# Twelve small triangular inverses on VectorE: each elimination step as two whole instructions instead of four halves

## The chip, the cores and the metric

One core of one Trainium2 chip runs the whole program. The metric is the device time of one execution in microseconds (us). On the core TensorE (PE in the profile, its weight loads PEld) does the matrix products and transposes, VectorE (DVE) and ScalarE (ACT) the elementwise work and the eviction of PSUM, GpSimd (POOL) some products and some DMA issues, and SyncE (SP) most DMA issues.

## The reference, cut to what matters

For 4 batches of 8 heads a state matrix of 40x40 is updated 768 times, and the outputs of all heads, joined to rows of 320, go through a two-layer block with a softmax gate and a normalisation:

```python
for t in range(S):                                   # S = 768
    y[:, :, t] = np.einsum('bhd,bhde->bhe', rt, state)
    Sa = np.einsum('bhde,bhe->bhd', state, at)
    state = state * wt[:, :, None, :] - np.einsum('bhd,bhe->bhde', Sa, bt) \
            + np.einsum('bhd,bhe->bhde', vt, kt)
x = y.transpose(0, 2, 1, 3).reshape(B * S, H * D)    # 3072 x 320
h = x @ w_in; sm = softmax(h); solu = h * sm
out = (layer_norm(solu) * g_ln) @ w_out
```

## The kernel before, in words

The recurrence is worked in chunks of C = 64 steps of time. A chunk of all heads of two batches is one unit of the loop: N = 24 units, index i, two for each of the 12 chunks of the sequence. Within a chunk the rank-one corrections are coupled by a matrix that is the identity plus a strictly triangular part of 64x64, one for each head and batch. The kernel inverts its two diagonal blocks of 32x32 (Q = 32) directly on VectorE, and joins the two by products on TensorE (`couple`, line 548, and `close`, line 561).

**The inverse** is `invert` (line 495). One call serves two units (GRP = 2), so there are 12 calls, called n = 0 to 11 here, each with 64 blocks laid over 128 partitions, so that each partition holds half of the 32 columns of a block. The off-diagonal entries are brought from a DRAM scratch by `spread` (line 488) into tile `blk`, the result grows in tile `uu`, 16 columns of 32 entries on each partition. Step j, for j = 1 to 30, adds entry j of every column begun so far, times row j of `blk`, to the entries j+1 to 31. There are n_c = (j+1)//2 such columns on a partition and m = 31 - j entries. For n_c below 4 (j = 1 to 6) a step is n_c instructions of line 508. From j = 7 on a step is a product into the scratch tile `prod` (line 516) and a sum into `uu` (line 519), both done on two halves of the columns: product of the first half, product of the second, sum of the first, sum of the second. A half has at most 72 elements on a partition, which is the width of `prod`; `prod` has two buffers. The last step is followed by two DMAs of `uu` to DRAM (line 525, on SP), from where `bring` (line 529) fetches each unit's part, `flip` (line 542) transposes it on VectorE, and `couple` uses it.

**The order of the work** is written out by hand, for all engines: every engine runs its instructions in the order in which the program issues them. `invert` is a generator that yields after each step j. The loop over i (line 971) hands out a few steps at a time, in gaps between VectorE's other work, by the strings in `plans` (line 896): `vector("o2 2")` (line 232) runs two steps for a unit that needs its inverse soon, and then two of any. `some` (line 870) counts the steps. From i = 12 on the plan repeats every two units: entries 24 and 25 of `plans`. The letters b, s and f in a plan are stages of a conversion of the weights from 64-bit floats (`split`, line 188: DVE lines 196 and 197, then ACT lines 199 to 206, then DVE lines 208 to 210), which is done in the first 140 us.

**VectorE's other work in a unit**, in its order: `aT` (line 427) and `bT` (line 440), which evict transposes from the PSUM pair called A that the next transposes (`pst`, `pb`) then use; some steps of an inverse; `lu` (line 444, from the solve `pu`); a step or two; `psi` and `lv` (line 444, from the scores `ps`); `flip`; eight or nine steps; the row maximum `nmax` (line 761) of the wide product `h`; `tot` (line 710); the weighing of `e` (line 777), after ACT's exponential (line 769); `st` and `x` (lines 721 and 724). ACT then squares `e` (line 790), evicts `kvT` (line 583) and the output rows `osb` (line 859), and PE goes on to the transposes of the next unit.

Of the kernel before, what the change touches and what calls it, by code (L numbers as in the profile page):

```python
# [9 lines left out]
FP32 = mybir.dt.float32  # L10
# [7 lines left out]
P = 128  # L18
# [35 lines left out]
def kernel(  # L54
# [31 lines left out]
    two = ctx.enter_context(tc.tile_pool(name="two", bufs=2))  # L86
# [401 lines left out]
    def spread(n):  # L488
        nb = two.tile([P, Q, Q], FP32, tag="blk", name="blk")
        for y in range(2):  # L490
            queue = nc.gpsimd if n else nc.sync
            queue.dma_start(out=nb[C * y:C * y + C], in_=blocks[n].rearrange("e b s c -> (e b) s c"))
        return nb

    def invert(n):
        u = two.tile([P, Q // 2, Q], FP32, tag="uu", name="uu")
        flat = u.rearrange("p c t -> p (c t)")
        nc.gpsimd.memset(u[C:P], 0.0)
        nc.gpsimd.memset(flat[C:P, 1::Q + 2], 1.0)
        nb = spread(n)  # L500
        yield
        nc.vector.tensor_tensor(out=u[0:C], in0=nb[0:C, 0::2], in1=above, op=ALU.mult)
        nc.vector.memset(flat[0:C, 0::Q + 2], 1.0)
        for j in range(1, Q - 1):
            m, n_c = Q - 1 - j, (j + 1) // 2
            if n_c < 4:
                for c in range(n_c):
                    nc.vector.scalar_tensor_tensor(out=u[:, c, j + 1:Q], in0=nb[:, j, j + 1:Q], scalar=u[:, c, j:j + 1],  # L508
                                                   in1=u[:, c, j + 1:Q], op0=ALU.mult, op1=ALU.add)
            else:  # L510
                parts_ = ((0, n_c // 2), (n_c // 2, n_c))
                ts = []
                for lo, hi in parts_:
                    prod = two.tile([P, 72], FP32, tag="prod", name="prod")
                    ts.append(prod[:, 0:(hi - lo) * m].rearrange("p (c r) -> p c r", c=hi - lo))
                    nc.vector.tensor_tensor(out=ts[-1], in0=nb[:, j:j + 1, j + 1:Q].to_broadcast([P, hi - lo, m]),  # L516
                                            in1=u[:, lo:hi, j:j + 1].to_broadcast([P, hi - lo, m]), op=ALU.mult)
                for x, (lo, hi) in zip(ts, parts_):
                    nc.vector.tensor_tensor(out=u[:, lo:hi, j + 1:Q], in0=u[:, lo:hi, j + 1:Q], in1=x, op=ALU.add)  # L519
            if j < Q - 2:  # L520
                yield
        inverse[n] = dram.tile([Q, C, Q], FP32, tag="uu_dram", name="uu_dram")
        for y in range(2):
            queue = nc.sync
            queue.dma_start(out=inverse[n][y::2].rearrange("c b t -> b c t"), in_=u[C * y:C * y + C])
        yield
# [352 lines left out]
    def begin_inverse(n):  # L879
        steps.append((n, invert(n)))  # L880
        next(steps[-1][1])
# [285 lines left out]
```

## Time and profile before

| what | value |
|---|---|
| three runs | 541.44, 537.95, 540.57 us; median 540.57 |
| the profiled execution | 538.14 us, of which its span is 536.0 |
| mean granted TensorE clock in the span | 0.962 |
| VectorE | 426.4 us busy, 1752 instructions |
| of these, line 516 (products) | 576, 105.4 us |
| of these, line 519 (sums) | 576, 105.3 us |
| chain of work that ended last | PE 76%, DVE 7%, ACT 5%, DMA 4% |

The span runs from the first to the last instruction of the program. A group of instructions is given with its count, its busy time in us and the mean duration of one in ns; then the idle time of its engine just before it, and what ended it. In a timeline a line is one instruction or several alike in a row: start, time from the first one's start to the last one's end, engine, line, operation, output and inputs, and in brackets the idle time before it and what ended it. Where two instructions of one engine overlap in the records, the second has started before the first one's result is written.

### The profile page before, as it was taken

The numbers are of one execution on the slowest core, as the hardware profiler recorded it, in microseconds if no ns is written. First come the engines' busy times: TensorE is split into PE (matmuls) and PEld (weight loads), VectorE is DVE, ScalarE is ACT, GpSimd is POOL, SyncE is SP. The second block draws the span as 40 slices with busy tenths as digits, with TensorE's granted clock in tenths as the row PEclk, the third lists the DMA queues.
The fourth block names the chain that finished last, engine by engine and source line by source line (L and its number), as shares of the span: only waits on it lengthen the run. The fifth ranks groups of instructions, "written<-read, shape, count | busy, mean of one in ns | idle before, by whom it ended". The sixth has DMA issues, their size and how long they took to land.

```text
span 536.0 us, 28052 instructions
## 1 busy us (share of the span) xinstructions
PE 480.8 (90%) x12029; PEld 392.5 (73%) x12029; DVE 426.4 (80%) x1752; ACT 314.5 (59%) x627; POOL 218.9 (41%) x368
## 2 busy tenths in 40 slices
PE   4634566888989999999999999999999999999997
PEld 3524555666878878877887887788778877887766
DVE  4596998999988987997988979979989788544322
ACT  3734466668467666666656665676656555654433
POOL 4545546244253434636355363545354321210300
PEclk9998577789999999999999999999999999999999
DMA  7998879766456566675775675675554451421210
GB/s 144 158 145 165 191 136 206 167 134 137 77 124 125 107 135 124 134 147 103 144 154 114 115 146 122 123 151 107 114 122 101 95 125 43 106 64 29 61 53 24
DMA packets 198315, 63.95 MB, mean 119 GB/s; under 512 B 170936, under 2 KB 190496, under 8 KB 198192
## 3 DMA queue, kind: packets, MB, share of 16 engines
q1 hardware_dynamic: 185456, 42.26, 41.8%
q0 software_dynamic: 10384, 19.30, 14.3%
q8 instruction: 94, 1.54, 1.2%
q10 hardware_dynamic: 2352, 0.62, 0.7%
q14 instruction: 29, 0.24, 0.2%
HBM read 47.96 MB, written 14.16 MB: 116 GB/s over the span
## 4 chain that ended last, share of the span: by engine, by line
PE 76%; DVE 7%; ACT 5%; DMA 4%; SPq 3%; issue 2%; ACTq 0%; POOL 0%; POOLq 0%; DVEq 0%
PE po L285 20%; PE h L285 18%; PE px L285 7%; PE py L285 6%; PE pyo L285 6%; PE ps L285 3%; PE pu L285 3%; PE plnT L804 2%; DMA raw_w<-in_w_dram 2%; PE pa L400 2%; SPq L311 2%; PE pb L400 2%; PE pkv L400 2%; PE psr L285 2%; PE pcum L285 1%
## 5 line engine op out<-in xcount | busy, mean ns | idle before, releaser
L285 PE MATMUL h<-w_in,xT 64*64 64x512 f32 (+1 forms) x1064 | 121.3, 552 | 0.0
L285 PE MATMUL po<-w,lnT 128*128 128x160 f32 x768 | 115.2, 304 | 0.0
L285 PEld LDWEIGHTS po<-w,lnT 128*128 128x128 f32 x768 | 105.5, 190 | 4.7 <-issue 0.8
L516 DVE TENSOR_TENSOR prod<-blk,uu 128x48 f32<-128x48 f32 (+19 forms) x576 | 105.4, 223 | 1.4
L519 DVE TENSOR_TENSOR uu<-uu,prod 128x48 f32<-128x48 f32 (+19 forms) x576 | 105.3, 223 | 0.0
L483 POOL DMA_DIRECT2D nt_dram<-nt x86 | 51.0, 599 | 83.4 <-ACT nt L475 82.0
L792 POOL TENSOR_TENSOR rs<-var,mhalf 128x1 f32<-128x1 f32 x24 | 15.8, 658 | 137.0 <-ACT var L791 137.0
L761 DVE TENSOR_REDUCE nmax<-h 128x1 f32<-128x1024 f32 x24 | 29.3, 1220 | 32.6 <-PE h L285 32.6
L285 PEld LDWEIGHTS h<-w_in,xT 64*64 64x64 f32 x1064 | 36.7, 134 | 19.1 <-issue 15.5
L790 ACT ACTIVATE sq<-e,mu 128x1024 f32<-128x1024 f32 x24 | 26.9, 1119 | 23.9 <-DVE e L777 23.9
L444 DVE TENSOR_TENSOR lu<-pu,cst 128x512 f32<-128x512 f32 x24 | 16.5, 687 | 27.5 <-PE pu L285 27.2
L769 ACT ACTIVATE e<-h,nmax 128x1024 f32<-128x1024 f32 x24 | 26.7, 1111 | 17.1 <-DVE nmax L761 16.9
L558 ACT ACTIVATE wy<-py,cst 128x256 f32<-128x256 f32 x24 | 11.4, 474 | 40.3 <-PE py L285 40.3
L311 POOL DMA_DIRECT2D raw_r<-in_r_dram x48 | 33.3, 699 | 0.6 <-issue 0.6
L777 DVE SCALAR_TENSOR_TENSOR e<-h,e 128x1024 f32<-128x1024 f32 x24 | 29.2, 1218 | 3.7 <-ACT e L769 3.4
L393 POOL TENSOR_TENSOR kb<-raw_b,inv 128x320 f32<-128x320 f32 x24 | 21.2, 882 | 25.4 <-DMA raw_b<-in_b_dram 18.0
L285 PEld LDWEIGHTS py<-tu,nt 64*64 64x64 f32 x768 | 17.3, 145 | 18.8 <-issue 14.2
L508 DVE SCALAR_TENSOR_TENSOR uu<-blk,uu 128x30 f32<-128x30 f32 (+3 forms) x144 | 28.6, 252 | 1.5 <-DMA blk<-nt_dram 0.9
L617 ACT COPY st<-psr 128x416 f32<-128x416 f32 (+1 forms) x44 | 14.2, 375 | 26.1 <-PE psr L285 24.9
L285 PE MATMUL pcum<-lw,cst 128*128 128x160 f32 x48 | 14.7, 450 | 16.4 <-ACT lw L351 16.4
L285 PEld LDWEIGHTS py<-aT,bT 40*64 40x64 f32 x768 | 16.7, 152 | 14.5 <-issue 8.7
L285 PE MATMUL px<-st,aT 40*64 40x104 f32 x704 | 21.9, 263 | 5.9 <-DVE lv L444 5.8
(152 smaller groups left out, 1096.8 us busy)
## 6 DMA issues: line engine op xcount, KB each, us to landing
xT<-x_dram SPq DMA_DIRECT2D x48, 160.0 KB, 3.9
blk<-nt_dram POOLq DMA_DIRECT2D x22, 256.0 KB, 3.4
raw_w<-in_w_dram SPq DMA_DIRECT2D x48, 80.0 KB, 3.0
a<-in_a_dram SPq DMA_DIRECT2D x48, 80.0 KB, 3.2
raw_r<-in_r_dram POOLq DMA_DIRECT2D x48, 80.0 KB, 3.9
lv<-in_v_dram SPq DMA_DIRECT2D x48, 80.0 KB, 3.3
out_dram<-osb SPq DMA_DIRECT2D x46, 80.0 KB, 3.4
raw_b<-in_b_dram SPq DMA_DIRECT2D x44, 80.0 KB, 4.8
```

The costliest lines, as they stand in the source:

```text
L285: nc.tensor.matmul(o, lhsT=lhsT, rhs=rhs, start=start, stop=stop, skip_group_check=True)
L311: queue.dma_start(out=x[half(p), :, 0:D], in_=ap[2 * bp + p, :, ci * C:(ci + 1) * C, :].rearrange("h t d -> t h d"))
L393: nc.gpsimd.tensor_tensor(out=kb[:, j:j + H, 0:D], in0=d["raw_" + n], in1=heads(d["inv"]), op=ALU.mult)
L400: nc.tensor.transpose(out=t[0:W2, p, at + C * j:at + C * j + C], in_=x[half(p), 2 * j:2 * j + 2].rearrange("p a b -> p (a b)")[:, skip:ski ...
L483: queue.dma_start(out=blocks[n][e].rearrange("(a x h) s c -> a x s h c", a=GRP, x=2)[at, x], in_=nt[home:home + Q].rearrange("p h j c -> p ...
L508: nc.vector.scalar_tensor_tensor(out=u[:, c, j + 1:Q], in0=nb[:, j, j + 1:Q], scalar=u[:, c, j:j + 1], in1=u[:, c, j + 1:Q], op0=ALU.mult, ...
L516: nc.vector.tensor_tensor(out=ts[-1], in0=nb[:, j:j + 1, j + 1:Q].to_broadcast([P, hi - lo, m]), in1=u[:, lo:hi, j:j + 1].to_broadcast([P, ...
L519: nc.vector.tensor_tensor(out=u[:, lo:hi, j + 1:Q], in0=u[:, lo:hi, j + 1:Q], in1=x, op=ALU.add)
L761: nc.vector.tensor_reduce(out=nmax, in_=d["h"], axis=AX.X, op=ALU.max, negate=True)
L769: nc.scalar.activation(out=e, in_=d["h"], func=AF.Exp, bias=d["nmax"], accum_out=d["esum"])
L777: nc.vector.scalar_tensor_tensor(out=d["e"], in0=d["h"], scalar=1.0 / DFF, in1=d["e"], op0=ALU.mult, op1=ALU.mult, accum_out=d["mu"])
L790: nc.scalar.activation(out=pair("A" if i == N - 2 else "h", "sq").rearrange("p a b -> p (a b)"), in_=d["e"], func=AF.Square, scale=-float( ...
```

## The change

For j = 7 to 30 the columns are no longer cut in halves. A step is one product over all n_c columns and one sum over all of them. The scratch tile becomes 136 elements wide, since the largest step has 128 (j = 15: 8 columns of 16). Steps 1 to 6, the order of the steps, the plans and all other instructions stay. An inverse has 48 instructions of lines 516 and 519 instead of 96.

```diff
             else:
-                parts_ = ((0, n_c // 2), (n_c // 2, n_c))
+                parts_ = ((0, n_c),)
                 ts = []
                 for lo, hi in parts_:
-                    prod = two.tile([P, 72], FP32, tag="prod", name="prod")
+                    prod = two.tile([P, 136], FP32, tag="prod", name="prod")
                     ts.append(prod[:, 0:(hi - lo) * m].rearrange("p (c r) -> p c r", c=hi - lo))
                     nc.vector.tensor_tensor(out=ts[-1], in0=nb[:, j:j + 1, j + 1:Q].to_broadcast([P, hi - lo, m]),
                                             in1=u[:, lo:hi, j:j + 1].to_broadcast([P, hi - lo, m]), op=ALU.mult)
                 for x, (lo, hi) in zip(ts, parts_):
                     nc.vector.tensor_tensor(out=u[:, lo:hi, j + 1:Q], in0=u[:, lo:hi, j + 1:Q], in1=x, op=ALU.add)
```

## The prediction

> **What bounds the kernel now.** I read the busy times and the costliest groups first, then the engines by stretches, then the chain of work that ended last, then VectorE's timeline around the steps.
>
> ```profile
> PE 480.8 (90%) x12029; PEld 392.5 (73%) x12029; DVE 426.4 (80%) x1752; ACT 314.5 (59%) x627; POOL 218.9 (41%) x368
> ...
> L516 DVE TENSOR_TENSOR prod<-blk,uu 128x48 f32<-128x48 f32 (+19 forms) x576 | 105.4, 223 | 1.4
> L519 DVE TENSOR_TENSOR uu<-uu,prod 128x48 f32<-128x48 f32 (+19 forms) x576 | 105.3, 223 | 0.0
> ```
>
> The steps are half of VectorE's busy time. By stretches:
>
> ```profile
> core 0: us, PE busy (x) PEld busy (x) DVE busy (x) ACT busy (x) POOL busy (x), PEclk, DMA share, GB/s
> ...
> 50.00:100.00 50.00, 31.81 (x877) 29.08 (x881) 45.94 (x203) 25.56 (x54) 23.53 (x37) 0.64 0.82 171
> ...
> 250.00:300.00 50.00, 49.73 (x1321) 41.58 (x1312) 46.18 (x193) 31.67 (x63) 25.17 (x39) 1.00 0.64 127
> ```
>
> From 50 to 150 us PE has gaps and VectorE nearly none. From 165 us PE has none; VectorE, though 92% busy, waits for PE: in each pair of units about 2.2 us ahead of `lu` and 0.7 to 0.95 us ahead of one `nmax`. So the change counts in full only in the first stretch. The chain there runs through the steps:
>
> ```profile
> 68.22 0.67 DVE aT L427
> 68.89 0.34 DVE scale L196
> ...
> 105.38 0.60 DVE aT L427
> ...
> 113.11 0.61 DVE lv L444
> 113.85 1.67 PE px L285 x32
> ```
>
> What a step costs is a matter of starts. The first four lines here are steps 10 and 11 of the last inverse; then, from inverse 1, line 210 of a weight conversion reads what line 209 has just written, and an unrelated step follows:
>
> ```profile
> 436.65 0.34 DVE L516 TENSOR_TENSOR prod<-blk,uu 128x42 f32<-128x42 f32 x2
> 436.91 0.34 DVE L519 TENSOR_TENSOR uu<-uu,prod 128x42 f32<-128x42 f32 x2
> 437.29 0.35 DVE L516 TENSOR_TENSOR prod<-blk,uu 128x60 f32<-128x60 f32 x2
> 437.56 0.34 DVE L519 TENSOR_TENSOR uu<-uu,prod 128x60 f32<-128x60 f32 x2
> ...
> 74.71 0.68 DVE L209 SCALAR_TENSOR_TENSOR w_in<-bits,w_in 128x512 f32<-128x512 uint16 x1
> 75.43 0.69 DVE L210 TENSOR_TENSOR w_in<-w_in,bits 128x512 f32<-128x512 f32 x1
> 76.04 0.28 DVE L516 TENSOR_TENSOR prod<-blk,uu 128x28 f32<-128x28 f32 x2
> ```
>
> The unrelated step starts 0.61 us after line 210, whose duration is 0.69: about 83 ns before its end (`lv` after `psi`, and most such neighbours, have the same). Line 210 starts 0.72 us after line 209: 35 ns after its end. A result needed at once thus costs 118 ns more. Today's halves hide that: each reads a result made two instructions earlier, and a step of four takes 0.26 + 0.27 = 0.53 us. Only after steps 10, 14, 18, 22 and 26, where the cut moves by a column, does the next product read the sum just made: 0.38 instead of 0.26 us at 436.91.
>
> **The change part by part.** It removes 576 VectorE instructions and doubles the size of the other 576.
>
> The product over all columns is read at once by the sum, and the sum at once by the next product. So a step takes 2 x (d + 35 ns), d the duration of a whole-size instruction. None of 73 to 128 elements is in the trace; the nearest rows of the same engine and type are these:
>
> ```profile
> L519 DVE TENSOR_TENSOR uu<-uu,prod 128x72 f32<-128x72 f32 x12 | 2.7, 222 | 0.0
> ...
> L721 DVE TENSOR_TENSOR st<-tot,ex 104x160 f32<-104x160 f32 x40 | 11.2, 322 | 0.0
> ```
>
> A line between them has 1.14 ns per element; I take it, as it brackets the sizes. The small sizes alone (7 elements 171 ns, 72 elements 222) give 0.78, the low end; 1.14 is also the high end, since line 710 with 416 elements at 581 ns gives no more. Step 11 (6 x 20 = 120 elements): d = 222 + 48 x 1.14 = 277, after 2 x 312 = 623 ns, before 532: +90. Step 10 paid one dependence already: 634 to 589, -45. Step 30 (15 elements): 391 to 421. Done for all 24 steps, 12.40 us becomes 13.69: +1.29 us an inverse; with 0.78 ns it is +0.80. Where a run of steps ends and another instruction follows that reads nothing of it, the last 118 ns fall away. In the steady plan (runs 7-13, 14, 15-18, 19-27, 28-30) that leaves +0.36, -0.02, +0.28, +0.34, -0.02 = +0.94 us of VectorE's time for each pair of units. [...]
>
> Now what of it lies on the path.
>
> Inverse 0 (30 to 45 us): VectorE then waits 3.95 us for `blk`, and SP issues the DMA of `uu` at 47.5, 2.2 us after the last step: hidden. Without that cover it would be 1.2 us.
>
> Inverse 1: steps 7 to 22 run in one piece up to `aT` at 68.2: +1.02 us, and the conversion behind it is late, for which ACT waits; ACT's queue is then full up to the product `py` at 72.8, for which PE waits.
>
> ```profile
> 69.26 0.72 ACT L199 ACTIVATE scale<-scale,top 128x512 int32<-128x512 int32 x1 [0.86 <-DVE scale L196]
> ...
> 224.43 0.53 ACT L859 ACTIVATE osb<-po,rs 128x320 f32<-128x320 f32 x1 [0.32 <-PE po L285]
> ...
> 261.70 0.53 ACT L859 ACTIVATE osb<-po,rs 128x320 f32<-128x320 f32 x1
> ```
>
> Inverse 2: step 7 alone before `psi`, -0.04. Steps 8 to 15 (+0.36) are covered by VectorE's waits of 1.57 us for `tu` and 0.39 for ACT. Steps 16 to 18 before `aT` at 105.3, +0.18 (the load for `pst` starts 0.05 us after `aT` ends). Steps 19 to 25 before `lu`, `psi`, `lv` and PE's `px` at 113.9, +0.36. Inverse 3: five steps at 135 to 139 us before `nmax`, +0.16. Sum of the first stretch: 1.68 us.
>
> Later, PE's order is met late only where ACT's `kvT` and `osb`, which follow the weighing of `e`, have no wait left; the two rows of `osb` show a unit with 0.32 us left and one with none, at 261.7, where PE's unit took 18.76 us instead of 18.46. Steps 7 to 14 make `e` later by +0.34. At 262 and 337 us (no wait left) that is 2 x 0.34 = 0.68; in the four such units with 0.32 left 0.02 each, 0.08; at 187 us `bT` ends 0.13 us before PE's `pst` load: +0.21. In the others (0.6 to 0.7 left) nothing. In the other half of a pair, +0.28 and +0.34 end at a VectorE wait of 0.66 to 0.95 us ahead of `nmax`, and what is left at the wait of 2.2 us ahead of `lu`. The `uu` DMAs, issued up to 0.1 us later, feed `flip` some 12 us later; one wait of 0.68 us for them is seen. The wider scratch costs no instruction; half the instruction records save nothing on PE's path.
>
> Sum: 1.68 + 0.97 = 2.65 us, about +0.5%. The profiled execution took 538.14 us (span 536.0 and 2.1 around it), so 540.8 by its own account and a span of 538.7. It lies 2.4 us below the median, so against the median: 540.57 + 2.65 = 543.2.
>
> **The rivals.**
>
> *Dependence is free, fewer instructions win (faster).* If the next instruction started 83 ns before the end whatever it reads, step 11 would take 2 x (277 - 83) = 387 ns instead of 532 and an inverse 8.0 us instead of 12.4. The first stretch would gain 0.58 us at 68 us (the weights' DMA lands at 68.2, which then ends the wait), 0.16 at 90, 0.42 at 105, 1.17 at 109 and 0.90 at 139; the late units at 262 and 337 would get their 0.27 each back: -3.8 us, 536.8. Against it stand the 0.72 us of lines 209 and 210 (all thirteen such pairs have 34 or 35 ns after the end) and the jump at step 10. [...]
>
> *More of GpSimd's stalls fall into the steps (slower).* 36 of the 1152 step instructions last about 0.67 to 1.3 us longer, while GpSimd runs `kb` (line 393, 0.88 us) or issues DMAs; four of them, 2.7 us, in most pairs of units. If a longer run of dependent instructions catches one more, 0.67 us, ahead of `e` in each such half, ACT is late by 0.69 in four units, 1.01 in two, 0.4 and 0.3 in two: 5.5 us, with the first stretch 7.2: 547.8. For it: VectorE has no slack in those halves. Against it: a stall ends with GpSimd's instruction and each `kb` makes at most two, so their count should be GpSimd's and not VectorE's. It decides from about one extra stall for each pair.
>
> *The granted clock.* Between 49 and 117 us the clock goes between full and half in pieces of 3.4 us or multiples. If VectorE's later results move three of them to half, with PE 73% busy (90 to 100 us), that is 3 x 3.4 x 0.73 / 2 = 3.7 us more: 546.9; it can as well go the other way.
>
> **How the numbers follow.** The forecast 0.62, free dependence 0.10, more stalls 0.20, the clock 0.08. The forecast's own range: at the low end of d about a third of the sum, 541.4, and with the runs' own scatter (-2.6, +0.9) 538.8 to 545. Together with the stalls' 547.8 and their scatter the range is 538.5 to 549.5. About 1% is what a measurement of this kernel can tell from no change. Faster by over 1% is half of free dependence, 0.05; slower the stalls and most of the clock, 0.25; within 1% 0.70.
>
> **What would show it.** Lines 516 and 519 with 288 instructions each; products of 120 elements near 277 ns and starts 312 ns apart; step 11 near 0.62 us. VectorE's busy time falls all the same, as 576 records with their overlaps go. `py` at 72.8 and `px` at 113.9 come 1.0 and 1.5 us later; PE's units after 165 us stay at 18.5 us but for those at 262 and 337. I am wrong if a sum starts before its product has ended, if the number of stalled steps changes, or if PE shows new waits for VectorE after 165 us.

## The result and the profile after

| | before | changed |
|---|---|---|
| median of 22 runs each, us | 541.38 (537.95 to 544.62) | 542.81 (539.8 to 545.94) |
| ratio, with its 95% interval | | 1.0031 [1.0017, 1.0046] |
| the same, later (12 runs against 35) | 539.48 | 541.67; 1.0045 [1.0024, 1.0066] |
| span of the profiled execution | 536.0 | 538.0 |

The change makes the kernel slower by 0.3 to 0.45%, about 2 us. The page of the changed kernel, lines of parts 1 and 5:

```profile
PE 479.5 (89%) x12029; PEld 390.3 (73%) x12029; DVE 422.8 (79%) x1176; ACT 314.4 (58%) x627; POOL 223.6 (42%) x368
...
L519 DVE TENSOR_TENSOR uu<-uu,prod 128x96 f32<-128x96 f32 (+17 forms) x288 | 85.6, 297 | 9.9
L516 DVE TENSOR_TENSOR prod<-blk,uu 128x96 f32<-128x96 f32 (+17 forms) x288 | 84.7, 294 | 8.2
```

576 instructions are gone and their busy time has fallen from 210.7 to 170.3 us; yet VectorE is later. The column behind the bar, idle time ahead of these lines, shows why: it was 1.4 and 0.0 us, and is 8.2 and 9.9. Busy time counts overlapping records once: before, the 576 records of line 516 add up to 128 us for 105.4 us of busy time. Before, they overlapped; now there are holes between them. The changed kernel's VectorE timeline in the last inverse, steps 10, 11 and the first half of 12:

```profile
438.67 0.27 DVE L516 TENSOR_TENSOR prod<-blk,uu 128x105 f32<-128x105 f32 x1
438.98 0.27 DVE L519 TENSOR_TENSOR uu<-uu,prod 128x105 f32<-128x105 f32 x1
439.28 0.28 DVE L516 TENSOR_TENSOR prod<-blk,uu 128x120 f32<-128x120 f32 x1
439.60 0.28 DVE L519 TENSOR_TENSOR uu<-uu,prod 128x120 f32<-128x120 f32 x1
439.92 0.28 DVE L516 TENSOR_TENSOR prod<-blk,uu 128x114 f32<-128x114 f32 x1
```

Each start is 0.03 us after the end of the one ahead: step 11 takes 0.64 us instead of 0.53, step 10, which paid one such wait before, 0.61 instead of 0.63. By the records, an instruction of 120 elements lasts 282 ns and the next starts 317 ns after its start (70 pairs; 34 or 35 ns after the end at every size). Summed over the starts, with the stalls beside GpSimd's work (see the rivals of the prediction) left out, the 24 steps take 13.4 us in the later inverses instead of 12.2.

By stretches, to be set against the rows of before:

```profile
50.00:100.00 50.00, 29.63 (x849) 26.27 (x853) 44.79 (x136) 24.53 (x52) 24.91 (x37) 0.67 0.83 172
250.00:300.00 50.00, 50.00 (x1346) 41.68 (x1338) 44.78 (x126) 31.26 (x64) 23.16 (x36) 1.00 0.65 129
```

PE does less in the first stretch (29.6 against 31.8 us of 50) and has no gap in the second, nearly as before (49.7). The chain of the changed kernel, and ACT's wait for the late conversion:

```profile
69.19 0.68 DVE aT L427
69.87 0.33 DVE scale L196
...
114.41 0.60 DVE psi L444
115.01 0.60 DVE lv L444
```

```profile
70.24 0.72 ACT L199 ACTIVATE scale<-scale,top 128x512 int32<-128x512 int32 x1 [2.77 <-DVE scale L196]
```

`aT` is 0.97 us later than in the profile of before, ACT's scaling 0.98, `lv` about 1.9. This compares one profile with one; the controls among the experiments say how far that goes. After 165 us the waits of VectorE for `h` have gone from 5.8 us to 1.7 (the two lines are of the kernel before, then of the changed one):

```profile
DVE nmax L761 <- PE h L285: 5.8, 7, 1.0
```

```profile
DVE nmax L761 <- PE h L285: 1.7, 7, 0.5
```

And the eviction of the output has no wait left in every late half of a pair. ACT's timeline in the unit at 300 us, first of the kernel before, then of the changed kernel, and PE's weight loads of the latter:

```profile
298.01 1.01 ACT L583 COPY kvT<-pkv 104x1024 f32<-104x1024 f32 x1 [0.37 <-PE pkv L400]
299.34 0.53 ACT L859 ACTIVATE osb<-po,rs 128x320 f32<-128x320 f32 x1 [0.32 <-PE po L285]
```

```profile
299.52 0.99 ACT L583 COPY kvT<-pkv 104x1024 f32<-104x1024 f32 x1
300.41 0.53 ACT L859 ACTIVATE osb<-po,rs 128x320 f32<-128x320 f32 x1
```

```profile
300.99 0.29 PEld L400 LDWEIGHTS pb<-cst,r 64*104 64x104 f32 x8 [0.21 <-ACT osb L859]
```

Where ACT waited 0.37 and 0.32 us for PE, it now waits for nothing, and PE waits 0.21 us for ACT. A table of all five late halves from 215 to 375 us (wait of ACT ahead of `kvT` plus that ahead of `osb`, us; in brackets PE's wait for `osb`, where there is one):

| kernel | 1st | 2nd | 3rd | 4th | 5th |
|---|---|---|---|---|---|
| before | 0.32 | 0 (0.21) | 0.69 | 0 (0.19) | 0.32 |
| before, once more | 0.32 | 0.32 | 0.66 | 0.10 | 0.32 |
| changed | 0 (0.21) | 0 (0.09) | 0 (0.21) | 0 (0.12) | 0 (0.07) |
| changed, once more | 0 (0.06) | 0 (0.06) | 0 (0.21) | 0 (0.21) | 0 (0.07) |

Of the runs told below, the two that make the change in the later inverses alone (e6, e12) have no wait in any of the five either. The two that make it in the first inverses alone (e5, e11) have one, of 0.31 to 0.64 us, in seven of ten.

### The profile page after: what moved, and what is told of

The parts are those of the page before. It is cut to its first block, busy times and chain, and to the rows that moved or that the text cites. A ratio compares the mean times of both kernels' runs of the same rounds, so it can differ in the third digit from the quotient of the medians.

```text
span 538.0 us, 27476 instructions
## 1 busy us (share of the span) xinstructions
PE 479.5 (89%) x12029; PEld 390.3 (73%) x12029; DVE 422.8 (79%) x1176; ACT 314.4 (58%) x627; POOL 223.6 (42%) x368
## 4 chain that ended last, share of the span: by engine, by line
PE 70%; DVE 14%; DMA 7%; ACT 3%; issue 3%; SPq 2%; POOL 1%; ACTq 0%; POOLq 0%; DVEq 0%
PE po L285 19%; PE h L285 17%; PE px L285 6%; PE py L285 6%; PE pyo L285 5%; PE ps L285 3%; PE pu L285 3%; DVE prod L516 2%; DVE uu L519 2%; PE plnT L804 2%; DMA blk<-nt_dram 2%; DMA raw_b<-in_b_dram 2%; DVE uu L508 2%; SPq L311 2%; PE psr L285 2%
## 5 line engine op out<-in xcount | busy, mean ns | idle before, releaser
L519 DVE TENSOR_TENSOR uu<-uu,prod 128x96 f32<-128x96 f32 (+17 forms) x288 | 85.6, 297 | 9.9
L516 DVE TENSOR_TENSOR prod<-blk,uu 128x96 f32<-128x96 f32 (+17 forms) x288 | 84.7, 294 | 8.2
L792 POOL TENSOR_TENSOR rs<-var,mhalf 128x1 f32<-128x1 f32 x24 | 18.0, 752 | 137.6 <-ACT var L791 137.6
L393 POOL TENSOR_TENSOR kb<-raw_b,inv 128x320 f32<-128x320 f32 x24 | 22.1, 920 | 26.5 <-DMA raw_b<-in_b_dram 19.2
L664 ACT ACTIVATE x<-px 128x832 f32<-128x832 f32 x24 | 20.7, 864 | 11.0 <-PE px L285 11.0
```

Of the source, the lines that this page charges most:

```text
L393: nc.gpsimd.tensor_tensor(out=kb[:, j:j + H, 0:D], in0=d["raw_" + n], in1=heads(d["inv"]), op=ALU.mult)
L664: return lambda: nc.scalar.mul(out=x0, in_=d["px"].rearrange("p h (j d) -> p h j d", j=4)[:, :, :, 0:W2], mul=-1.0)
```

## The experiments

All times are ratios to the kernel before, run on the same chip. The theory is that of the prediction: a result needed at once costs 118 ns, the whole-size steps pay it twice, and the path feels it in the first 165 us and where `e` is late. The rivals: only the number of instructions counts; or VectorE's total counts wherever it falls.

**Does dependence cost, with the same instructions?** Four runs, of edits of the kernel before or after that change no size.

e1, the halves in reverse order:

```diff
-                parts_ = ((0, n_c // 2), (n_c // 2, n_c))
+                parts_ = ((n_c // 2, n_c), (0, n_c // 2))
```

> The kernel before with the second half first, for the products and for the sums; the same instructions. A column that moves from the second to the first half (after steps 10, 14, 18, 22, 26) was then summed two instructions before it is read. Dependence theory: the five starts of 258 ns become about 140, 0.59 us less of VectorE's time for an inverse; on the path three of them in inverse 1, one in inverse 2, one in inverse 3, and one in each late unit: 0.6 us in the first stretch and some 0.3 later, ratio to before 0.998 to 1.000. Count theory (a result needed at once costs nothing, only the number of instructions counts): nothing changes anywhere, the five starts stay as they are, ratio 1.000.

Measured: 0.9995 [0.9969, 1.0021]. Its VectorE timeline at steps 10 and 11:

```profile
438.83 0.34 DVE L516 TENSOR_TENSOR prod<-blk,uu 128x63 f32<-128x63 f32 x2
439.09 0.34 DVE L519 TENSOR_TENSOR uu<-uu,prod 128x63 f32<-128x63 f32 x2
439.35 0.35 DVE L516 TENSOR_TENSOR prod<-blk,uu 128x60 f32<-128x60 f32 x2
```

The jump of 0.38 us after step 10 is 0.26. An inverse takes 11.8 us without stalls, 0.4 less and not 0.59: in the repeating plan steps 14 and 18 end a run and had nothing to pay. The time does not tell it from no change. So the count theory falls here on the trace and not on the time.

e2 and e3, the sum right behind its product, in the inverses 0 to 3 or 4 to 11 (`n < 4`, `n >= 4`):

```diff
                     nc.vector.tensor_tensor(out=ts[-1], in0=nb[:, j:j + 1, j + 1:Q].to_broadcast([P, hi - lo, m]),
                                             in1=u[:, lo:hi, j:j + 1].to_broadcast([P, hi - lo, m]), op=ALU.mult)
+                    if n < 4:
+                        nc.vector.tensor_tensor(out=u[:, lo:hi, j + 1:Q], in0=u[:, lo:hi, j + 1:Q], in1=ts.pop(), op=ALU.add)
```

> The kernel before, in inverses 0 to 3 alone in the order product, sum, product, sum on the halves, so that each sum reads the product just made; the number and the size of the instructions stay. Dependence theory: two starts of d + 35 instead of d - 83 ns in each step, about +0.21 us a step and +4.9 us an inverse; on the path 16 steps of inverse 1 (3.4 us), 11 of inverse 2 (2.3), five of inverse 3 (1.1), and up to 2.5 of inverse 0, whose DMA then goes out late: 7 to 9.5 us, ratio 1.013 to 1.018. Count theory: ratio 1.000.

> The same order in inverses 4 to 11 alone. Dependence theory: +4.9 us for each pair of units against some 3.0 to 3.3 us for which VectorE waits in a pair. If those waits can take up any lateness, 1.7 us a pair is left, 13 us in eight pairs, ratio 1.024. If only the waits count that lie behind the late results (the theory of the prediction: ACT's kvT and osb in one half, the wait ahead of nmax in the other), 1.2 us is left in one half and about 1.6 in the other, 20 us, ratio 1.037. Count theory: ratio 1.000.

Measured: 1.0294 [1.0252, 1.0335] and 1.0581 [1.0536, 1.0626]. With not one instruction more, larger or smaller, the kernel is 16 and 31 us slower: the count theory is out. The timeline of e3:

```profile
266.19 0.22 DVE L519 TENSOR_TENSOR uu<-uu,prod 128x60 f32<-128x60 f32 x1
266.33 0.21 DVE L516 TENSOR_TENSOR prod<-blk,uu 128x60 f32<-128x60 f32 x1
266.58 0.22 DVE L519 TENSOR_TENSOR uu<-uu,prod 128x60 f32<-128x60 f32 x1
266.71 0.21 DVE L516 TENSOR_TENSOR prod<-blk,uu 128x57 f32<-128x57 f32 x1
```

From a sum to a product that reads none of it, 0.13 to 0.14 us; from the product to its own sum 0.25. Both times went well above what was expected. An inverse took 17.7 us without stalls, 5.5 more and not 4.9, but most of the miss is in the waits. In e2 the expectation let 7 to 9.5 us of the four inverses' 22 reach the end, and 16 did. In e3 some 4 us of each pair's 5.5 reached it (31 us of the times and 34.5 of the profile, over eight pairs), though VectorE waits for 3 us in a pair of the kernel before. The wait ahead of `lu` was hardly drawn on, as the line of e3 for 165 to 430 us shows (total, times, longest):

```profile
DVE lu L444 <- PE pu L285: 11.0, 6, 2.4
```

That is 1.8 us in most pairs, where the kernel before has 2.2: PE comes later to `pu` too.

The wait for a result is not the cost in itself. In the profile of before, all 576 sums carry a wait on VectorE's own semaphore (the counter that its instructions raise), and yet start 47 to 93 ns before the end of the instruction ahead. In that of the changed kernel all 288 carry it too, and start 33 to 35 ns after that end. What costs is that the result waited for is the newest one.

e4, the changed kernel without the dependences. The product reads columns of `blk`, the sum adds rows of `blk`; the inverses are left out by this:

```diff
-                                            in1=u[:, lo:hi, j:j + 1].to_broadcast([P, hi - lo, m]), op=ALU.mult)
+                                            in1=nb[:, lo:hi, j:j + 1].to_broadcast([P, hi - lo, m]), op=ALU.mult)
                 for x, (lo, hi) in zip(ts, parts_):
-                    nc.vector.tensor_tensor(out=u[:, lo:hi, j + 1:Q], in0=u[:, lo:hi, j + 1:Q], in1=x, op=ALU.add)
+                    nc.vector.tensor_tensor(out=u[:, lo:hi, j + 1:Q], in0=u[:, lo:hi, j + 1:Q], in1=nb[:, lo:hi, j + 1:Q], op=ALU.add)
```

> The changed kernel, with the product reading columns of blk instead of the columns just summed, and the sum adding rows of blk instead of the product: the same 576 instructions of the same sizes, but none reads what the one ahead of it wrote. The inverses are left out by this. Dependence theory: starts d - 83 apart, 200 ns at 120 elements, an inverse 8 us instead of 13.7; VectorE then has slack everywhere; 3.8 us less than before, ratio 0.991 to 0.995. Count theory: the starts are those of the changed kernel (317 ns at 120 elements), ratio to before 1.003.

Measured: 0.9893 [0.9858, 0.9928], a little more gain than was expected. Its timeline at steps 11 and 12:

```profile
248.13 0.27 DVE L516 TENSOR_TENSOR prod<-blk 128x120 f32<-128x120 f32 x1
248.32 0.27 DVE L519 TENSOR_TENSOR uu<-uu,blk 128x120 f32<-128x120 f32 x1
248.52 0.27 DVE L516 TENSOR_TENSOR prod<-blk 128x114 f32<-128x114 f32 x1
```

The same sizes start 0.19 to 0.20 us apart instead of 0.32. So neither the size nor the wider scratch, which e4 has too, is what costs: without its dependences the change would be worth 4 to 8 us. In its profile 3.5 of the 4.0 us gained lie ahead of 170 us; after that PE's units take what they took.

**Where the loss lies.** e5 and e6 make the change for a part of the inverses, e11 and e12 are the same two once more:

```diff
-                parts_ = ((0, n_c // 2), (n_c // 2, n_c))
+                parts_ = ((0, n_c),) if n < 4 else ((0, n_c // 2), (n_c // 2, n_c))
```

> The change in inverses 0 to 3 alone (steps of the first 163 us), the scratch 136 wide; inverses 4 to 11 on halves as before. Theory of the prediction: 1.7 of its 2.65 us lie here, on VectorE's own chain: ratio to before 1.003. Rival, that the first stretch gives its lateness back, since the clock and GpSimd's stalls decide there (the profile of the changed kernel is 1.9 us late at 111 us and only 0.3 at 132): 1.000 to 1.001.

> The change in inverses 4 to 11 alone. Theory of the prediction: 1.0 us, in the units where ACT's eviction has no wait left: 1.002. Rival: all of the loss is here, 1.6 us, 1.003, since VectorE's total is what counts; the order with a dependence in each pair showed 4.3 us a pair of units for 5.4 us more of VectorE's work, which speaks for this.

> The change in inverses 0 to 3 alone, a second time, to narrow the interval: 1.002 by the first time, 1.003 by the prediction's term for the first stretch (1.68 us), 1.000 if all of the loss comes later.

> The change in inverses 4 to 11 alone, a second time: 1.004 by the first time, 1.002 by the prediction's term for the stretch after 165 us (0.97 us).

Measured, early: 1.0020 [0.9997, 1.0043] and 1.0002 [0.9978, 1.0026]; late: 1.0040 [1.0018, 1.0063] and 1.0016 [0.9987, 1.0044]. The means, 1.0011 and 1.0028 (0.6 and 1.5 us), add up to the whole change. The late part is clear of no change in one of its two runs, the early part in neither. Two controls say how far a single profile can go:

> The kernel before, once more, as a control: ratio 1.000. Its profile shows how far the starts of PE's units in the first 163 us move from one execution to the next with nothing changed. If by 1 us and more, a single profile cannot place the 1.7 us of the first stretch; if by less than 0.5 us, the giving back seen between 111 and 132 us in the changed kernel belongs to the change.

> The changed kernel once more: 1.003 as before. In its profile: whole-size instructions 34 or 35 ns apart, about 37 stalled ones, and after 165 us the same 1.0 to 1.5 us lost as in the first profile, if that loss is not chance.

Measured: 1.0008 [0.9987, 1.0029] and 1.0045 [1.0024, 1.0066]. Start of PE's product `pu` in four units, from the records, as difference to the first profile of before (us):

| kernel | 107 us | 170 us | 376 us | 497 us | from 170 to 376 | from 170 to 497 |
|---|---|---|---|---|---|---|
| before, once more | -0.5 | -1.1 | -1.5 | -1.6 | -0.4 | -0.6 |
| changed | +1.5 | +0.5 | +1.2 | +2.0 | +0.7 | +1.5 |
| changed, once more | +1.4 | +1.1 | +2.5 | +3.0 | +1.4 | +1.9 |
| early part (e5, e11) | +0.7, +0.9 | +1.5, -0.6 | +1.7, -0.6 | +1.9, +0.1 | +0.2, 0.0 | +0.5, +0.7 |
| late part (e6, e12) | +2.7, +1.2 | +3.4, +0.8 | +4.8, +2.1 | +5.4, +2.7 | +1.4, +1.3 | +2.1, +1.9 |
| halves in reverse order (e1) | +1.5 | +1.8 | +2.0 | +3.1 | +0.2 | +1.3 |

Two executions of the same kernel differ by 1.1 us at 170 us; e6, which changes nothing there, is 2.7 late at 107. So the stretch ahead of 165 us cannot be read from one profile, and the giving back between 111 and 132 us, seen in one, proves nothing. From 170 to 497 us the kernels whose later steps are those of before scatter from -0.6 to +0.7 us, and e1, whose inverses are shorter, loses 1.3; so the 1.5 to 2.1 us of the changed kernels are not all theirs. From 170 to 376 us the two groups do not meet: -0.4 to +0.2 us with the halves, e1 among them, and +0.7 to +1.4 with whole steps. In this window a loss of about 1.2 us is shown.

That VectorE's total counts wherever it falls is out as well. Each of the eight later inverses got 1.2 us longer, 10 us in all, and 1.5 us came out; in e4 each got 4 us shorter, and after 170 us that gained 0.5, which is within the scatter.

**Can the late part be mended?** e9 and e10 move step 14 in the repeating plan, on the changed kernel and on e1:

```diff
-        24: ("o2 2", "", "", "o9", "o4", "", ""),
-        25: ("1", "2", "2", "8", "1", "", ""),
+        24: ("o2 3", "", "", "o9", "o4", "", ""),
+        25: ("1", "2", "2", "8", "", "", ""),
```

> The changed kernel with one step (step 14) moved in the repeating plan from ahead of the weighing of e in the late half of each pair to ahead of lu in the other half. Theory: the changed kernel loses after 165 us because e is late in every pair (no wait left ahead of kvT and osb in all five pairs from 220 to 370 us, where the kernel before has that in two); the move makes e 0.62 us earlier there, and the other half has 0.17 ahead of nmax and 0.5 to 0.7 at kvT and osb to take it. So osb gets 0.3 us of wait back in the late half, and some 1 to 1.5 us of the loss after 165 us goes: ratio to before 1.000 to 1.002. Rival, that VectorE's total decides: nothing gained, ratio 1.003 to 1.004, since the total stays.

> The kernel before with the halves in reverse order (0.4 us less of VectorE's time for an inverse) and the same move of step 14: the version that may beat both. Theory: no unit after 165 us in which ACT's osb is late, 0.5 us gained there, and up to 0.6 in the first stretch: ratio 0.997 to 0.999. Rival, that what is left of the late units is not worth anything: 1.000.

Measured: 1.0022 [1.0000, 1.0045] and 0.9999 [0.9973, 1.0025]. e9 failed in what it should show: `osb` got no wait back in the late half. Step 14 runs behind `nmax`, and `e` needs ACT's exponential of `nmax`; with the step gone VectorE waited 0.28 us for that instead, and `nmax` itself stayed late. I had moved the wrong step. The time lies between those of the theory and of the rival and settles neither. e10 had such waits in three of five halves (0.36 to 0.66 us), where e1 without the move has them in four, and no time gained that can be told. No version beat the kernel before.

## Why the prediction was right, and which terms were not

The sign held, and so did the mechanism of a step. That the times lie so near (543.2 against 542.8) is in part luck. The median of the three runs that the forecast starts from lies 0.8 us below that of the 22, and the loss was 1.7 [0.9, 2.5] and 2.4 [1.3, 3.6] us for the 2.65 forecast, with a first term that came out smaller and a second that came out larger. By its steps:

- *What a step costs.* Right: starts 34 or 35 ns after the end at every size. The size was a little low: 282 ns at 120 elements instead of 277, and 291 at 128 instead of 286.
- *An inverse.* 13.4 us in the repeating plan, where the prediction's 13.69 less the last 118 ns of each of the five runs is 13.1. Before it was 12.2, as reckoned (12.40 less the two dependences after steps 14 and 18, where a run ends). So it is +1.2 for the +0.94. Run 7-13 with its stalls left out went from 3.7 to 4.2 us, +0.46 and not +0.36. The term missed is d, some 6 ns low on average over the 48 instructions.
- *The first stretch, 1.68 us.* 0.6 by e5 and e11, with an interval of about -0.3 to 1.5; 1.0 and 1.6 by the two profiles against the mean of the two before, which themselves differ by 1.1. Too large by the times, and by them not even clear of nothing: the size is open, and so is which of its four inverses pays. That inverse 0 is hidden was not tried by itself; in e2, where it takes 5.5 us more, PE was 2.5 late at 66 us in one profile, no more than is left over the 2.2 us of cover.
- *After 165 us, 0.97 us.* Probably too small: about 1.2 us by the profiles from 170 to 376 us, where nearly all of its units lie, and 1.5, with an interval of about 0.5 to 2.5, by the times of e6 and e12. The mechanism held, but in all five late halves and not at 262 and 337 us alone. The prediction let the lateness of `e` end in waits of 0.32 to 0.69 us, as they stood in one profile, and took 0.34 us where the steps alone bring 0.46. By the records, `lu` starts 1.23 us after PE's `pu` in the late halves of both kernels, so that VectorE carries nothing over from the half ahead. `nmax` starts 10.26 to 10.99 us after `pu` in the two profiles of before, in seven of ten late halves 10.26 or 10.27, and 10.81 to 11.15 in the two of the changed kernel. That is at least 0.54 us later than in a quiet half of before, and three late halves that had slack lost it. What adds to the 0.46 is open. In the other half the lateness did end at the wait ahead of `nmax`, as predicted: at least 0.16 us of its 0.66 to 1.0 is left.
- *The signs named ahead.* `py` came 1.0 us later and `px` 1.9, for the 1.0 and 1.5 predicted; in the second profile of before `py` is 1.4 us earlier, so this says little. Two of the signs of being wrong came. The stalled steps went from 34 to 37, and PE has new waits behind a late `e` after 165 us, such as the 0.21 us at 301. The second is the late term, mis-sized as said.
- *Free dependence.* Out by e2, e3 and e4. In this case fewer instructions, each waiting for the last, are slower by 0.1 us in a step of 120 elements (0.64 us for 0.53).
- *What free dependence would give.* The 3.8 us worked out for it are near what e4 shows once dependence is really gone: 4.0 in the profile, 5.8 [3.9, 7.7] in the times. That is in part luck: e4 also loses most of GpSimd's stalls, which the sum did not have.
- *More of GpSimd's stalls.* Out: 37 stalled step instructions (over 100 ns longer than the median of their size) in both profiles of the changed kernel and 34 in both of before (36 in the prediction's count), but less time above those medians in all, 22.1 and 22.2 us against 22.9 and 23.5.
- *The granted clock.* Not needed. Ahead of 165 us it was at half of full speed for 41 us in both profiles of before, for 38 and 20 in those of the changed kernel, which were equally late at 107 us.

## What to carry to other kernels

Where an engine's records overlap, as VectorE's do here (by about 83 ns where the second reads nothing of the first, while one that reads it starts 34 or 35 ns after its end), put an independent instruction between a write and its read. One was enough here: halves of 60 elements read a result 0.26 us after the start of the instruction that makes it, which lasts 0.21. Where a step is cut in halves, see in the starts whether the halves hide that, before they are joined: busy time and the number of instructions both fell here while the engine got later. And a wait seen in one profile is not a store that can be drawn on. It serves only what is late ahead of it, and it moves along when the result waited for comes later too: in e3 1.8 of the 2.2 us ahead of `lu` stayed unused.

## What was not expected

GpSimd's stalls depend here on where VectorE's steps lie, not on how many there are: 34 of 1152 step instructions were stalled before, 37 of 576 in the changed kernel. In e4, where the steps are done or nearly done when GpSimd starts `kb` (the last one ahead of `nmax` ends at 249.4 us and `kb` starts at 250.7; the last one ahead of `lu` starts at 259.60 and `kb` at 259.62), 4 of 576 are stalled, for 1.8 us in all, instead of 34 for 23.5. A shorter inverse may thus be worth more than its own starts say; no run tried that apart.

And the waits give back little: some 4 of 5.5 us more work in a pair came out at the end in e3, on an engine that had waited 3 us in that pair.
